# A transformer block on one core: buffer clearing moved to another engine, LayerNorm order pinned, and the feed-forward LayerNorm pulled ahead of each segment

## The chip, the cores and the metric

One core of a Trainium2 chip. TensorE (PE) multiplies matrices, with its weight loads (PEld) beside it; VectorE (DVE), ScalarE (ACT) and GpSimd (POOL) do elementwise work, and SyncE (SP) issues most of the transfers. ACT and POOL also issue transfers of their own. The metric is the device time of one execution in microseconds; lower is better. An execution takes 657.92 us before the change (median of four).

## The reference

Inputs are bfloat16: x of 2048 tokens by 576, 32 heads of 18, weights wq, wk, wv, wo (576 x 576), w1 (576 x 4608), w2 (4608 x 576). The core of it:

```python
for s in range(4):                       # four segments of L = 512 tokens
    logits = einsum('bhqd,bhkd->bhqk', qs, ks) * scale + causal_mask
    a_dot = einsum('bhqk,bhkd->bhqd', softmax(logits), vs)
    pq = phi(qs)                         # phi(t) = t + 1 if t > 0 else exp(t)
    a_mem = einsum('bhld,bhde->bhle', pq, M) / (einsum('bhld,bhd->bhl', pq, z)[..., None] + 1e-06)
    o = g * a_mem + (1.0 - g) * a_dot    # g = sigmoid(beta), one value per head
    M = M + einsum('bhld,bhle->bhde', phi(ks), vs);  z = z + einsum('bhld->bhd', phi(ks))
# q, k, v = layernorm(x) @ wq, wk, wv
h = x + concat(o) @ wo
out = h + gelu(layernorm(h) @ w1 + b1) @ w2 + b2
```

## The kernel before

**Two phases, tiles of 128 tokens.** Phase A is attention, over 16 tiles T (four a segment). Phase B is the feed-forward network (FFN), over four segments b of 512 tokens. The rows of h pass between them through `h_dram` in DRAM.

**A projection tile** (`proj_tile`): DVE takes the statistics of the tile (two `bn_stats`, one `bn_aggr`, tiles `stats` and `mv`), POOL makes `ve` (variance plus epsilon) and `rstd` (its power of -0.5), DVE makes `nmr` and then `xn`, the normalised tile. PE transposes it (`pT`), DVE copies that out, and 30 matmuls into six PSUM tiles `pq` give Q, K and V. ACT casts these into `Qp`, `Kp` (a head takes 32 columns, of which 18 are filled and the rest must be zero) and `Vp`. DVE makes relu and min of K for the memory; PE transposes Q (`ptq`) and K (`ptk`), DVE copies them to `QTt` and `KT`, and four DVE copies spread QTt into a block-diagonal `QTbd` whose other blocks must be zero. From segment 1 on, Q also meets the memory `BDp`, which gives `Rsb`.

**An attention tile** (`attention_tile`): for each pair of (head group, key tile) PE makes scores into `st` (two PSUM buffers), ACT takes the exp into `E`, POOL masks the diagonal blocks (`affine_select`), and PE multiplies with V into `pv`. `normalize` divides and adds Rsb, on DVE, into `oseg`. `wo_tile` transposes oseg, copies it (`oT`), multiplies with `wo_sb` into `ph`, adds x and writes h to DRAM.

**Order.** The code emits projections of tiles 0 to 2, then for each T: attention of T, projection of T+3, `wo_tile` of T-1. A scheduler of the framework then orders the instructions of each engine by its own estimate; each engine runs its list in order. Xn, Qp, Kp, QTbd and the FFN weights w1 and w2 are cut out of one SBUF array, so all of these are called `arena` in the profile. The zero parts are cleared once at the start, before anything is projected: Qp, Kp and two of the five QTbd buffers on DVE, three QTbd buffers and `expKp` on POOL (L132 to L143); the masks, wo's padding and oseg's padding follow on POOL (L145 to L179). ACT issues the loads of wq, beta and wo, POOL that of wk, SP that of x and wv.

**FFN.** For each segment b, and for its four tiles: load `h_t`, POOL adds the bias b2 (`hb`), DVE and POOL do the LayerNorm (`statsB`, `mvB`, `veB`, `rstdB`, `nmrB`, `hn`), PE transposes five blocks (`pT3`, printed as pT), DVE copies them into `hnT`. Then 36 ft blocks of five matmuls each, two blocks to a PSUM tile `pf` and one gelu on ACT (`g2`, printed g), then four tiles of 72 matmuls into `acc`, which DVE adds to hb and SP stores.

Of the kernel before, what the change touches and what calls it, by code (L numbers as in the profile page):

```python
# [11 lines left out]
ALU = mybir.AluOpType  # L12
# [12 lines left out]
def kernel(  # L25
# [15 lines left out]
    cfg = {"mask": "pool", "bd_eng": "dve", "ahead": 3, "wo_lag": 1}  # L41
# [27 lines left out]
    MASK = cfg.get("mask", "dve")  # L69
    PJ_BUFS = cfg.get("pj_bufs", 3)  # L70
    PV_BUFS = cfg.get("pv_bufs", 1)
    HB_ENG = cfg.get("hb_eng", "pool")
    BD_ENG = cfg.get("bd_eng", "pool")
# [7 lines left out]
    PROJ_E = NCH * 3 * D + 2 * DPAD + 4 * H * 32 + 2 * TPS * H * 32 + 2 * NCH * P + 4 * NG * P + (cfg.get('ahead', 1) + 2) * NG * 4 * P  # L81
# [13 lines left out]
    nc.gpsimd.memset(negh[:], -0.5)  # L95

    with ExitStack() as phA:
# [7 lines left out]
        epool = phA.enter_context(tc.tile_pool(name="epool", bufs=cfg.get("e_bufs", 8 if cfg.get("half_su", True) else 4)))  # L105
        psS = phA.enter_context(tc.tile_pool(name="psS", bufs=cfg.get("st_bufs", 2 if cfg.get("half_su", True) else 1), space=PSUM))
# [3 lines left out]
        NB = 2  # L110
# [9 lines left out]
        AHEAD = cfg.get("ahead", 1)  # L120
        NQ = AHEAD + 2
        QTbd_t = [carve(NG * 4 * P).rearrange("p (g j n) -> p g j n", g=NG, j=4) for _ in range(NQ)]

# [3 lines left out]
        queues = [nc.scalar, nc.gpsimd, nc.sync]  # L127
        for i, w in enumerate((A_wq, A_wk, A_wv)):
            eng = queues[i]
            eng.dma_start(wqkv[:, 0:4, i * D:(i + 1) * D], w[0:512, :].rearrange("(c p) n -> p c n", p=P))  # L130
            eng.dma_start(wqkv[0:64, 4, i * D:(i + 1) * D], w[512:576, :])
        nc.gpsimd.memset(wqkv[64:128, 4, :], 0.0)  # L132
        for i in range(NB):
            nc.gpsimd.memset(xn_t[i][:, D:DPAD], 0.0)
        for i in range(NB):
            nc.vector.memset(Qp_t[i][:], 0.0)
            nc.vector.memset(Kp_t[i][:], 0.0)
        for i in range(NQ):
            (nc.gpsimd if i % 2 == 0 else nc.vector).memset(QTbd_t[i][:], 0.0)  # L139
        Vp_t = [persX.tile([P, TPS, H, 19], BF16, name=f"Vp{i}") for i in range(NB)]  # L140
        for i in range(NB):
            nc.gpsimd.memset(Vp_t[i][:, :, :, 18:19], 1.0)
        nc.gpsimd.memset(expKp[:], 0.0)  # L143
        mask01 = consts.tile([P, P], BF16, name="mask01")
        nc.gpsimd.memset(mask01[:], 1.0)  # L145
        nc.gpsimd.affine_select(out=mask01[:], in_=mask01[:], pattern=[[1, P]], compare_op=ALU.is_ge,
                                fill=0.0, base=0, channel_multiplier=-1)
        maskneg = None
        if MASK == "pe":
            maskneg = consts.tile([P, P], BF16, name="maskneg")  # L150
            nc.gpsimd.memset(maskneg[:], 0.0)
            nc.gpsimd.affine_select(out=maskneg[:], in_=maskneg[:], pattern=[[1, P]], compare_op=ALU.is_ge,
                                    fill=-1.0e9, base=0, channel_multiplier=-1)
        bdmask = consts.tile([P, 4 * 19], F32, name="bdmask")
        nc.gpsimd.memset(bdmask[:], 1.0)
        bdv = bdmask[:, :].rearrange("p (j e) -> p j e", e=19)
        nc.gpsimd.affine_select(out=bdv, in_=bdv, pattern=[[-32, 4], [0, 19]], compare_op=ALU.is_ge,
                                fill=0.0, base=0, channel_multiplier=1)
        nc.gpsimd.affine_select(out=bdv, in_=bdv, pattern=[[32, 4], [0, 19]], compare_op=ALU.is_ge,
                                fill=0.0, base=17, channel_multiplier=-1)  # L160
        wo_sb = wX.tile([P, NCH, D], BF16, name="wo_sb")
        nc.gpsimd.memset(wo_sb[64:128, 4, :], 0.0)
        beta_sb = consts.tile([P, H], BF16, name="beta_sb")
        nc.scalar.dma_start(beta_sb[:], A_beta.partition_broadcast(P))
        nc.scalar.dma_start(wo_sb[:, 0:4, :], A_wo[0:512, :].rearrange("(c p) n -> p c n", p=P))
        nc.scalar.dma_start(wo_sb[0:64, 4, :], A_wo[512:576, :])
        G = consts.tile([P, H], F32, name="G")
        OMG = consts.tile([P, H], F32, name="OMG")
        Mst = consts.tile([P, NG, 76], F32, name="Mst")
        nc.scalar.activation(G[:], beta_sb[:], ACT.Exp, scale=-1.0)  # L170
        nc.vector.tensor_scalar_add(G[:], G[:], 1.0)
        nc.vector.reciprocal(G[:], G[:])
        nc.vector.tensor_scalar(out=OMG[:], in0=G[:], scalar1=-1.0, scalar2=1.0, op0=ALU.mult, op1=ALU.add)

        state = {}
        NO = 3
        oseg_t = [persX.tile([P, DPAD], BF16, name=f"oseg{i}") for i in range(NO)]
        for i in range(NO):
            nc.gpsimd.memset(oseg_t[i][:, D:DPAD], 0.0)  # L179
        qtp = phA.enter_context(tc.tile_pool(name="qtp", bufs=AHEAD + 2))  # L180
        rpool = phA.enter_context(tc.tile_pool(name="rpool", bufs=AHEAD + 2))
# [6 lines left out]
        def proj_tile(s, t):  # L188
# [4 lines left out]
            if t == 0:  # L193
# [8 lines left out]
            tcols = slice(t * P, (t + 1) * P)  # L202
            stats = small.tile([P, 2, 6], F32, name="stats")
            nc.vector.bn_stats(out=stats[:, 0, :], in_=x_seg[:, t, 0:288])
# [10 lines left out]
            nc.vector.tensor_scalar(out=xn[:, 0:D], in0=x_seg[:, t, :], scalar1=rstd[:, 0:1],  # L215
                                    scalar2=nmr[:, 0:1], op0=ALU.mult, op1=ALU.add)
# [21 lines left out]
            if s < NSEG - 1:  # L238
                nc.vector.tensor_scalar_max(reluKp[:, t, :], Kp[:], 0.0)
# [9 lines left out]
            for j in range(4):  # L249
                eng = nc.gpsimd if BD_ENG == "pool" else nc.vector  # L250
                eng.tensor_copy(QTbd[32 * j:32 * j + 32, :, j, :], QTt[32 * j:32 * j + 32, :, :])  # L251
# [34 lines left out]
        def mupdate(s):  # L286
            Vp = Vp_t[s % NB]
# [22 lines left out]
        HALF = cfg.get("half_su", True)  # L310

        def attention_tile(s, t):
            T = s * TPS + t
            QTt = state[("QT", T)]
# [3 lines left out]
            oseg = oseg_t[T % NO]  # L318
            bcols = [(g, kt) for g in range(NG) for kt in range(t + 1)]
            SUs = [bcols[i:i + 4] for i in range(0, len(bcols), 4)]  # L320
# [20 lines left out]
            def do_pv(g):  # L341
# [4 lines left out]
                for j in range(4):  # L346
                    h = 4 * g + j
                    hl = h - 16 * hf
                    for kt in range(t + 1):
                        E, b, slot = E_of[(g, kt, j)]  # L350
# [29 lines left out]
            for L in pairs:  # L380
# [6 lines left out]
                for b, (g, kt) in enumerate(L):  # L387
# [8 lines left out]
                    for j in range(4):  # L396
                        E_of[(g, kt, j)] = (E, b, j)
                for g in pending:
                    do_pv(g)
# [175 lines left out]
```

## Time and profile before

| | us |
|---|---|
| median of 4 runs (657.4 to 659.84) | 657.92 |
| the profiled execution | 659.19 |
| its span in the trace | 657.5 |
| mean granted clock of TensorE in it | 0.955 |

A row of the profile's groups reads: line, engine, operation, output <- input (partitions x elements, type), count | busy time in us, mean ns of one | idle time of the engine just before, and what ended it. A row of the timeline reads: start, duration (both us), engine, line, operation, count, and in brackets how long the engine had been idle before and what ended that. A row of the chain reads: start, duration, engine, tile, line, count. A row of a window reads: its limits and length, then the busy us (and count) of PE, PEld, DVE, ACT and POOL, the granted clock, the busy share of the DMA engines and their GB/s.

### The profile page before, as it was taken

The page shows a single profiled execution, that of the slowest core. Times are in us where ns is not written, and L with a number is a line of the kernel's source. Part 1 is how long each engine was busy: PE and PEld are TensorE (multiplying, and loading weights), DVE is VectorE, ACT ScalarE, POOL GpSimd, SP SyncE. Part 2 cuts the span into 40 slices and gives each one's busy share as a digit, 9 for nine tenths or more (in the row PEclk, how much of TensorE's full clock was granted, in tenths as well). Part 3 has the DMA queues.
Part 4 walks back from the last instruction along what each step waited for, and adds up shares of the span by engine and source line. Part 5 has one row for each costly group of instructions (what it writes and reads, how often), then busy time and mean ns, then how long its engine had stood idle before and what let it go on. Part 6 is the DMA issues. An engine that isn't in the chain of part 4 may idle for free.

```text
span 657.5 us, 11656 instructions
## 1 busy us (share of the span) xinstructions
PE 555.5 (84%) x4935; PEld 354.4 (54%) x4992; DVE 244.0 (37%) x630; ACT 285.4 (43%) x355; POOL 161.7 (25%) x249
## 2 busy tenths in 40 slices
PE   0488988899988897687069999799997999989997
PEld 0356555566556555453034477345773457744576
DVE  6578674877567736642361000400103001010011
ACT  0156889768966895586024400144001440034300
POOL 9642334422442234632640001200111000000000
PEclk9979999999989998898569999899997999999999
DMA  7010010000001024950310000000000000000000
GB/s 252 0 37 2 19 37 20 19 20 20 19 19 44 19 74 133 322 189 12 99 45 1 0 10 19 28 0 1 10 19 10 0 1 10 19 10 0 1 19 19
DMA packets 19190, 25.98 MB, mean 40 GB/s; under 512 B 1665, under 2 KB 17841, under 8 KB 19137
## 3 DMA queue, kind: packets, MB, share of 16 engines
q1 hardware_dynamic: 16258, 17.93, 8.8%
q0 software_dynamic: 1520, 5.97, 2.6%
q10 hardware_dynamic: 1360, 1.34, 0.6%
q8 instruction: 39, 0.64, 0.4%
q14 instruction: 13, 0.11, 0.1%
HBM read 20.51 MB, written 4.72 MB: 38 GB/s over the span
## 4 chain that ended last, share of the span: by engine, by line
PE 69%; DVE 16%; POOL 6%; ACT 6%; issue 2%; DMA 1%; SPq 0%; DVEq 0%; ACTq 0%; POOLq 0%
PE pf L527 24%; PE acc L537 22%; PE pq L226 8%; ACT E L386 5%; DVE arena L251 5%; PE st L383 5%; PE ph L417 4%; PE pv L351 3%; POOL arena L139 2%; DVE QTt L59 2%; DVE KT L59 1%; POOL hb L498 1%; DVE arena L262 1%; DVE hnT L59 1%; PE ptq L245 1%
## 5 line engine op out<-in xcount | busy, mean ns | idle before, releaser
L386 ACT ACTIVATE E<-st 128x1024 bf16<-128x1024 f32 x160 | 155.5, 1023 | 41.8 <-PE st L383 19.1
L527 PE MATMUL pf<-hnT,arena 128*128 128x512 bf16 x704 | 160.4, 387 | 4.0 <-DVE hnT L59 2.8
L530 ACT ACTIVATE g<-pf 128x1024 bf16<-128x1024 f32 x72 | 73.6, 1024 | 205.1 <-PE pf L527 205.0
L537 PE MATMUL acc<-arena,g 128*128 128x288 bf16 x1152 | 142.9, 286 | 0.0
L537 PEld LDWEIGHTS <-g 128*128 128x128 bf16 x1152 | 112.6, 98 | 30.4
L394 POOL TENSOR_SCALAR_AFFINE_SELECT E<-E 128x512 bf16<-128x512 bf16 x128 | 85.5, 679 | 150.6 <-ACT E L386 150.2
L527 PEld LDWEIGHTS <-arena 128*128 128x128 bf16 x720 | 71.8, 100 | 91.4 <-issue 10.7
L542 DVE TENSOR_TENSOR o_t<-acc,hb 128x288 bf16<-128x288 f32 x32 | 13.2, 453 | 279.2 <-PE acc L537 279.2
L383 PE MATMUL st<-arena,KT 128*128 128x512 bf16 x279 | 88.6, 384 | 13.0 <-ACT E L386 9.7
L351 PEld LDWEIGHTS <-E 128*128 128x128 bf16 x1280 | 49.9, 96 | 48.2 <-POOL E L394 16.8
L226 PE MATMUL pq<-arena 128*128 128x288 bf16 x480 | 72.9, 297 | 1.3 <-DVE arena L59 1.0
L351 PE MATMUL pv<-Vp,E 128*128 128x19 bf16 x1280 | 59.8, 173 | 10.8 <-ACT E L386 6.4
L226 PEld LDWEIGHTS <-arena 128*128 128x128 bf16 x480 | 46.4, 101 | 17.6 <-DVE arena L59 3.1
L498 POOL TENSOR_TENSOR hb<-h_t,b2bc 128x576 f32<-128x576 bf16 x16 | 20.4, 1281 | 137.0 <-DVE o_t L542 131.5
L57 ACT CAST arena<-pq 128x288 bf16<-128x288 f32 x64 | 24.5, 408 | 27.0 <-PE pq L226 27.0
L251 DVE COPY arena<-QTt 32x1024 bf16<-32x1024 bf16 x64 | 35.3, 551 | 0.6
L383 PEld LDWEIGHTS <-KT 128*128 128x128 bf16 x320 | 25.4, 97 | 17.4 <-issue 8.1
L417 PE MATMUL ph<-wo_sb,oT 128*128 128x288 bf16 x160 | 30.0, 311 | 3.3 <-DVE oT L59 2.4
L519 PE MATMUL pT<-ident,hn 128*128 128x128 bf16 x80 | 8.7, 250 | 26.8 <-DVE hnT L59 13.6
L219 PE MATMUL pT<-ident,arena 128*128 128x128 bf16 x80 | 7.5, 224 | 25.2 <-POOL rstd L211 24.5
L417 PEld LDWEIGHTS <-oT 128*128 128x128 bf16 x160 | 15.3, 105 | 13.8 <-DVE oT L59 7.3
L519 PEld LDWEIGHTS <-hn 128*128 128x128 bf16 x80 | 6.6, 111 | 29.1 <-issue 23.5
(91 smaller groups left out, 427.0 us busy)
## 6 DMA issues: line engine op xcount, KB each, us to landing
arena<-in_B_w_dram POOLq DMA_DIRECT2D x3, 864.0 KB, 5.3
arena<-in_B_w_dram SPq DMA_DIRECT2D x3, 864.0 KB, 10.3
x_seg<-in_A_x_dram SPq DMA_DIRECT2D x4, 576.0 KB, 4.7
xr<-in_A_x_dram SPq DMA_DIRECT2D x16, 144.0 KB, 2.8
h_dram<-h_sb SPq DMA_DIRECT2D x16, 144.0 KB, 1.8
arena<-in_B_w_dram POOLq DMA_DIRECT2D x3, 768.0 KB, 8.4
arena<-in_B_w_dram SPq DMA_DIRECT2D x3, 768.0 KB, 8.6
h_t<-h_dram SPq DMA_DIRECT2D x16, 144.0 KB, 2.2
```

What stands on the lines that cost most here:

```text
L59: nc.vector.tensor_copy(out_ap, in_ap)
L226: nc.tensor.matmul(pq[:], lhsT=xnT[:, c, :], rhs=wqkv[:, c, c0:c0 + 288], start=(c == 0), stop=(c == NCH - 1))
L251: eng.tensor_copy(QTbd[32 * j:32 * j + 32, :, j, :], QTt[32 * j:32 * j + 32, :, :])
L351: nc.tensor.matmul(pv[:, hl, 0:19], lhsT=E[:, b, slot * P:(slot + 1) * P], rhs=Vp[:, kt, h, :], start=(kt == 0), stop=(kt == t))
L383: nc.tensor.matmul(st[:, b, :], lhsT=KT[:, g, kt * P:(kt + 1) * P], rhs=QTbd[:, g, :, :], start=True, stop=True)
L386: nc.scalar.activation(E[:], st[:], ACT.Exp, scale=SCALE)
L394: nc.gpsimd.affine_select(out=v, in_=v, pattern=[[0, 4], [1, P]], compare_op=ALU.is_ge, fill=0.0, base=0, channel_multiplier=-1)
L417: nc.tensor.matmul(ph[:], lhsT=oT[:, c, :], rhs=wo_sb[:, c, hf * 288:(hf + 1) * 288], start=(c == 0), stop=(c == NCH - 1))
L498: nc.gpsimd.tensor_tensor(out=hb[:], in0=h_t[:], in1=b2bc[:], op=ALU.add)
L527: nc.tensor.matmul(pf[:, k, :], lhsT=w1_sb[:, c, ft * P:(ft + 1) * P], rhs=hnT[:, c, :], start=(c == 0), stop=(c == NCH - 1))
L530: nc.scalar.activation(g2[:], pf[:], ACT.Gelu_apprx_tanh)
L537: nc.tensor.matmul(acc[hf][:], lhsT=gT[ft // 2][:, ft % 2, t * P:(t + 1) * P], rhs=w2_sb[:, ft, hf * 288:(hf + 1) * 288], start=(ft == 0), ...
```

## The change

Four things move; what is computed stays.

1. **Start.** The zero fills of Qp, Kp, expKp, four and a half QTbd buffers go to ACT, as `memzero` (an activation on the buffer taken as 32-bit words); POOL keeps half of the first QTbd. wq and wv are loaded by SP, wk by POOL. Masks, the sigmoid of beta, wo's load and the pads are emitted where they are first used. A first power on POOL (`warm`) is done right at the start.
2. **LayerNorm order in attention.** The first statistics instruction of a tile and its xn get an issue-order token: the statistics of tile T+1 stand behind the xn of tile T on DVE.
3. **FFN LayerNorm ahead.** `ffn_prep(b)` does what phase B's LayerNorm did, from its own load `h_ln` of h. For b = 0 it is called inside phase A, from T = 13 on in the code's order; for b + 1 between the two matrix products of segment b. `load_hb(b)` loads h a second time for the residual and bias.
4. **Pools.** hn and hnT get pools outside of phase A; the pool of g2 gets `reuse_waits="tile"`.

```diff
-    cfg = {"mask": "pool", "bd_eng": "dve", "ahead": 3, "wo_lag": 1}
+    cfg = {"wqueues": "sgs", "prologue": 3, "prep_in_a": 1}
...
+    hnTp = ctx.enter_context(tc.tile_pool(name="hnTp", bufs=2))
...
+    warm = consts.tile([P, 2], F32, name="warm")
+    nc.gpsimd.memset(warm[:], 1.0)
+    nc.gpsimd.tensor_tensor(out=warm[:, 1:2], in0=warm[:, 0:1], in1=negh[:], op=ALU.pow)
+    hn_t = [consts.tile([P, DPAD], BF16, name=f"hn{i}") for i in range(2)]
+    hnT_of = {}
+    def ffn_prep(b, spool, wpool, pspool, pstag, first_use):
+        hnT = hnTp.tile([P, NCH, LSEG], BF16, name="hnT")
+        hnT_of[b] = hnT
+        for t in range(TPS):
+            T = b * TPS + t
+            h_t = wpool.tile([P, D], BF16, name="h_ln")
+            nc.sync.dma_start(h_t[:], h_dram[T])
...
-        queues = [nc.scalar, nc.gpsimd, nc.sync]
+        qmap = {"s": nc.sync, "a": nc.scalar, "g": nc.gpsimd}
...
-        for i in range(NB):
-            nc.vector.memset(Qp_t[i][:], 0.0)
-            nc.vector.memset(Kp_t[i][:], 0.0)
-        for i in range(NQ):
-            (nc.gpsimd if i % 2 == 0 else nc.vector).memset(QTbd_t[i][:], 0.0)
...
-        nc.gpsimd.memset(expKp[:], 0.0)
...
+            if T < NB:
+                nc.gpsimd.memset(xn[:, D:DPAD], 0.0)
+                nc.scalar.memzero(Qp[:])
+                nc.scalar.memzero(Kp[:])
+            if T == 0 and ST_MODE == "bd":
+                nc.scalar.memzero(QTbd_t[0][:, 0:4, :, :])
+                nc.gpsimd.memset(QTbd_t[0][:, 4:8, :, :], 0.0)
+                for k in range(1, NQ):
+                    nc.scalar.memzero(QTbd_t[k][:])
+                if NSEG > 1:
+                    done.add("expKp")
+                    nc.scalar.memzero(expKp[:])
...
+            if LN_TOK:
+                tc.stamp_issue_order_token(bn0.ins, "ln")
...
+            if LN_TOK:
+                tc.stamp_issue_order_token(xn_ins.ins, "ln")
...
         def attention_tile(s, t):
+            if once("attn_setup"):
...
+                nc.scalar.dma_start(beta_sb[:], A_beta.partition_broadcast(P))
+                nc.scalar.activation(G[:], beta_sb[:], ACT.Exp, scale=-1.0)
...
+        emit_proj_upto(cfg.get("prologue", 1))
         for T in range(NT):
             s, t = divmod(T, TPS)
             attention_tile(s, t)
-            if T + AHEAD < NT:
-                emit_proj(T + AHEAD)
+            emit_proj_upto(T + AHEAD + 1)
             if T - WO_LAG >= 0:
-                wo_tile(T - WO_LAG)
+                emit_wo(T - WO_LAG)
+            if T >= PREP_FROM:
+                maybe_prep()
...
+        prep_b(0)
+        for b in range(NSEG):
+            hnT = hnT_of[b]
+            hb_tiles = load_hb(b)
...
                 nc.scalar.activation(g2[:], pf[:], ACT.Gelu_apprx_tanh)
                 gT.append(g2)
+            prep_b(b + 1)
             for t in range(TPS):
```

The order that the scheduler makes, at the places where it counts. First ACT at the start of the program. Before:

```order
L130 DMA arena<-in_A_wq_dram 128x4x576
L131 DMA arena<-in_A_wq_dram 64x576
L164 DMA beta_sb<-in_A_beta_dram 128x32
L165 DMA wo_sb<-in_A_wo_dram 128x4x576
L166 DMA wo_sb<-in_A_wo_dram 64x576
L170 ACT_TABLE_LOAD
L170 ACTIVATE G<-beta_sb 128x32
L57 CAST arena<-pq 128x16x18 x4
```

and after, from the table load to the first casts:

```order
L228 ACTIVATE arena<-arena 128x2048 x4
L231 ACTIVATE arena<-arena 128x2048
L222 ACTIVATE arena<-arena 128x512
L223 ACTIVATE arena<-arena 128x512
L361 DMA beta_sb<-in_A_beta_dram 128x32
L468 DMA wo_sb<-in_A_wo_dram 128x4x576
L362 ACTIVATE G<-beta_sb 128x32
L469 DMA wo_sb<-in_A_wo_dram 64x576
L57 CAST arena<-pq 128x16x18 x4
```

The fills (L222 to L231; two of 512 words and one of 1024 stand ahead of the rows shown) now come before the load of beta, the sigmoid's exp (G) and the first casts of Q and K.

Second, DVE in the middle of attention, behind an xn (the row `arena<-x_seg,rstd,nmr`; rden, c and oseg belong to `normalize`). Before:

```order
L59 COPY arena<-pT 128x640
L215 TENSOR_SCALAR arena<-x_seg,rstd,nmr 128x576
L327 RECIPROCAL rden<-pv 128x16
L213 TENSOR_SCALAR nmr<-mv,rstd 128x1
L329 TENSOR_TENSOR c_1023<-rden,OMG 128x16
L332 TENSOR_TENSOR oseg_149<-pv,c_1023 128x288
```

and after:

```order
L59 COPY arena<-pT 128x640
L249 TENSOR_SCALAR arena<-x_seg,rstd,nmr 128x576
L235 BN_STATS stats<-x_seg 128x6
L382 RECIPROCAL rden<-pv 128x16
L241 BN_AGGR mv<-stats 128x2
L239 BN_STATS stats<-x_seg 128x6
L384 TENSOR_TENSOR c_1032<-rden,OMG 128x16
L247 TENSOR_SCALAR nmr<-mv,rstd 128x1
L387 TENSOR_TENSOR oseg_120<-pv,c_1032 128x288
L124 BN_STATS statsB<-h_ln 128x6
L125 BN_STATS statsB<-h_ln 128x6
L127 BN_AGGR mvB<-statsB 128x2
```

Each tile's statistics now stand directly behind the xn of the tile before, where they used to be taken for several tiles at once and earlier; the FFN's statistics (statsB) have come into attention.

Third, PE where attention passes into the FFN. Before, the last of the 20 transposes of segment 0 stand directly ahead of the first pf, behind the last output projection:

```order
L519 LDWEIGHTS hn_5083
L519 MATMUL pT_5174<-ident,hn_5083 128x128
L519 LDWEIGHTS hn_5083
L519 MATMUL pT_5174<-ident,hn_5083 128x128
L527 LDWEIGHTS arena
L527 MATMUL pf<-hnT,arena 128x512
```

and after, the first pf stand among the last pv:

```order
L406 LDWEIGHTS E
L406 MATMUL pv<-Vp_117,E 128x19
L596 LDWEIGHTS arena
L596 MATMUL pf<-hnT,arena 128x512
L596 LDWEIGHTS arena
L596 MATMUL pf<-hnT,arena 128x512
L596 LDWEIGHTS arena
L596 MATMUL pf<-hnT,arena 128x512
L406 LDWEIGHTS E
L406 MATMUL pv<-Vp_117,E 128x19
```

Behind these come 13 pv, 8 pf, the three last transposes of oseg, 3 pf, the ten ph of the last tile, and 166 pf to the first acc. The transposes of segment 0 now lie inside attention, and those of the next segments stand in fives between the first acc of the segment before, with five acc in between.

More of the change, by code (lines that the diff above doesn't have):

```diff
@@ L143 @@
-        nc.gpsimd.memset(expKp[:], 0.0)
[L144 to L173, printed above, removed]
-        state = {}
[L176 to L179, printed above, removed]
@@ L481, with prep_b, load_hb @@
         nc.vector.tensor_copy(b2bc[:], b2tmp[:])
-        NBh = 2
-        hn_t = [persB.tile([P, DPAD], BF16, name=f"hn{i}") for i in range(NBh)]
-        for i in range(NBh):
-            nc.gpsimd.memset(hn_t[i][:, D:DPAD], 0.0)
-            nc.gpsimd.memset(hn_t[i][:, D:D + 1], 1.0)
-        for b in range(NSEG):
-            hnT = workB.tile([P, NCH, LSEG], BF16, name="hnT")
-            hb_tiles = []
+        def prep_b(b):
+            if b < NSEG and b not in hnT_of:
+                ffn_prep(b, smallB, lnB, psT, None, first_use=(len(hnT_of) == 0))
+        def load_hb(b):
+            tiles = []
             for t in range(TPS):
```

260 lines of the change are left out of this document (164 added, 96 removed).

## The prediction

> **What bounds the kernel now.** I read the page's busy shares and slices first, then the chain of waits, then three stretches of the timeline.
>
> ```profile
> PE 555.5 (84%) x4935; PEld 354.4 (54%) x4992; DVE 244.0 (37%) x630; ACT 285.4 (43%) x355; POOL 161.7 (25%) x249
> PE   0488988899988897687069999799997999989997
> PEclk9979999999989998898569999899997999999999
> PE 69%; DVE 16%; POOL 6%; ACT 6%; issue 2%; DMA 1%; SPq 0%; DVEq 0%; ACTq 0%; POOLq 0%
> ```
>
> PE is busy 84% of the span and carries 69% of the chain. Its slices are low in three kinds of places: at the very start, at slices 18 to 20 (296 to 345 us), and in single slices later. The change works on exactly these, so I price each from its own rows.
>
> **The start.** Timeline rows (start, duration, engine):
>
> ```profile
> 0.97 0.48 DVE L136 MEMSET arena<- 128x512 uint32 x1 [0.97 <-PEq L559]
> 3.32 1.53 POOL L132 MEMSET arena<- 64x1728 bf16 x1
> 5.08 10.45 POOL L139 MEMSET arena<- 128x4096 bf16 x3
> 22.08 0.74 POOL L209 TENSOR_SCALAR ve<-mv 128x1 f32<-128x1 f32 x4
> 22.79 2.13 POOL L211 TENSOR_TENSOR rstd<-ve,negh 128x1 f32<-128x1 f32 x4
> 24.52 0.71 PE L219 MATMUL pT<-ident,arena 128*128 128x128 bf16 x5 [24.52 <-POOL rstd L211]
> 25.90 4.97 PE L226 MATMUL pq<-arena 128*128 128x288 bf16 x30 [0.67 <-DVE arena L59]
> 27.32 0.40 ACT L57 CAST arena<-pq 128x288 bf16<-128x288 f32 x1 [16.05 <-PE pq L226]
> 34.32 0.82 PE L383 MATMUL st<-arena,KT 128*128 128x512 bf16 x2 [1.89 <-DVE arena L251]
> ```
>
> PE first works at 24.52, because the LayerNorm of tile 0 waits for POOL, and POOL clears buffers until 22 us. The first Q/K/V eviction (the cast) stands at 27.32, the first score matmul at 34.32, 7.0 us later. The change clears the same buffers on ACT instead: four of 512 four-byte words, one of 1024, five of 2048 in each partition. No row shows such a fill; the nearest give a straight line:
>
> ```profile
> L386 ACT ACTIVATE E<-st 128x1024 bf16<-128x1024 f32 x160 | 155.5, 1023 | 41.8 <-PE st L383 19.1
> L57 ACT CAST arena<-pq 128x288 bf16<-128x288 f32 x64 | 24.5, 408 | 27.0 <-PE pq L226 27.0
> 8.31 1.28 ACT L170 ACT_TABLE_LOAD   x1 [8.31 <-DMA arena<-in_A_wq_dram]
> xr<-in_A_x_dram SPq DMA_DIRECT2D x16, 144.0 KB, 2.8
> ```
>
> From 288 to 1024 elements is 0.615 us, so 0.836 ns an element and 0.17 us fixed: 0.60, 1.02 and 1.88 us for the three sizes, 4 x 0.60 + 1.02 + 5 x 1.88 = 12.8 us. DVE begins its first fill at 0.97, with nothing of the program ahead of it; if ACT does the same and loads its table in 1.28 us, it has cleared at 15.0. Behind that stands the load of beta (the order puts it there), and the sigmoid's exp waits for it: 2.8 us as for a quiet transfer, then 0.2 for the exp and 0.5 to issue the last wo load, so the first cast comes at 18.5 instead of 27.32, **a gain of 8.8 us**. PE is not later than that: POOL keeps the weights' pad (to 4.9), half of one buffer (10.45 / 3 / 2 = 1.7) and small things of about 0.8 ahead of the variance and the power (0.2 and 0.5 by the x4 rows), so rstd is there at 8.1 instead of 23.3, and pq, which now stands 2.6 behind it, can start near 11, three PSUM buffers ahead of the casts. From cast to first score I keep the 7.0 us. The moves of wq and wv onto SP, and of wo behind the fills, cost nothing: the casts come later than a 2.8 us transfer needs, and wo is needed only by the first output projection, behind a whole attention tile. Bounds: if a four-byte word costs ACT twice as much, the cast comes at 31.3 and the start loses 4.0 us; if something hides the fills entirely, pq at 11 instead of 25.9 is worth 14.9 us. I take the line between the two ACT rows, the nearest; DVE's 0.48 for 512 words says that such a fill needn't be slower.
>
> [...]
>
> **The handover to the FFN.** Timeline rows, and from the chain in order of time those with matmul counts and no bracket:
>
> ```profile
> 306.67 0.49 PE L351 MATMUL pv<-Vp,E 128*128 128x19 bf16 x13 [0.52 <-POOL E L394]
> 308.19 0.46 DVE L338 TENSOR_TENSOR oseg<-a,Rsb 128x288 bf16<-128x288 f32 x1
> 318.25 3.76 POOL L498 TENSOR_TENSOR hb<-h_t,b2bc 128x576 f32<-128x576 bf16 x3 [5.41 <-DMA h_t<-h_dram]
> 309.24 0.49 DVE L59 COPY oT<-pT 128x640 bf16<-128x640 bf16 x1 [0.60 <-PE pT L410]
> 309.79 2.58 PE L417 MATMUL ph<-wo_sb,oT 128*128 128x288 bf16 x10 [0.58 <-DVE oT L59]
> 335.48 0.58 PE L527 MATMUL pf<-hnT,arena 128*128 128x512 bf16 x1 [1.03 <-DVE hnT L59]
> 135.88 1.31 PE ph L417 x10
> 429.81 10.74 PE pf L527 x49
> 376.57 35.46 PE acc L537 x287
> ```
>
> Attention ends at 307.2, yet the first FFN matmul (pf) starts at 335.5: h goes to DRAM and back, POOL adds the bias ahead of the LayerNorm of four tiles, and PE is idle for most of 28 us. Then 180 pf run until the second FFN product (acc) starts at 376.57. In the change, segment 0's LayerNorm, transposes and hnT are done inside attention, so pf needs only a PSUM pair that the exp releases, and weights that landed earlier: DMA is down to 59 GB/s at 290 to 295 us (below). Working forward on the order's rows, at 10.74 / 49 = 0.219 us for each pf: pv ends at 307.2; 8 pf to 308.9; 3 transposes of oseg (it is ready at 308.65) to 309.4; 3 pf while DVE copies oT, to 310.1; ph x10 at 1.31 to 311.4; 166 pf at 36.4 to 347.8. I add 1.0 for the gelu table load and a slow clock, 348.8. **376.6 - 348.8 = 27.8 us gained.** Bounds: ph at its 2.58 us of the slow clock and 14 pf at double time leave 23; no addition at all leaves 29.
>
> **The three segment boundaries.** Four chain rows, of which the first stands above:
>
> ```profile
> 457.60 35.46 PE acc L537 x287
> 539.52 35.46 PE acc L537 x287
> 618.35 35.46 PE acc L537 x287
> 413.33 0.44 PE L519 MATMUL pT<-ident,hn 128*128 128x128 bf16 x5 [1.13 <-DVE hnT L59]
> 576.28 0.44 PE L519 MATMUL pT<-ident,hn 128*128 128x128 bf16 x5 [0.91 <-DVE hnT L59]
> ```
>
> From the end of one acc run to the start of the next is 45.6, 46.5 and 43.4 us; 180 pf take 39.5 of each, which leaves 6.1 + 7.0 + 3.9 = 17.0 us. There PE does 20 transposes and waits in between for DVE's copy and the next hn. The change puts the same transposes, in fives, between the first acc matmuls of the segment before, and DVE has its first two hn ready long since. Each five cost 0.44 us; five acc take 0.62 us (35.46 / 287 each), against DVE's copy and hn, so about 2.0 us a boundary. **17.0 - 6.0 = 11.0 us gained.** Bounds: no cover at all, 3 x 3.9, leaves 5.3; free transposes give 17.0.
>
> ```profile
> 416.90:421.00 4.10, 4.04 (x11) 1.54 (x12) 2.46 (x9) 0.06 (x1) 0.98 (x3) 0.58 0.04 13
> 498.40:502.40 4.00, 3.75 (x9) 1.43 (x10) 0.31 (x1) 0.00 (x0) 0.00 (x0) 0.50 0.02 4
> 579.30:583.00 3.70, 3.60 (x16) 1.66 (x17) 0.00 (x0) 1.02 (x1) 0.00 (x0) 1.00 0.00 0
> 290.00:295.00 5.00, 4.32 (x53) 2.28 (x51) 1.88 (x6) 4.46 (x5) 1.85 (x3) 1.00 0.20 59
> ```
>
> In these stretches (busy time by engine, then granted clock, DMA share, GB/s) the clock after the first two boundaries was 0.58 and 0.50, after the third 1.00; that is why the third costs 3.9 and not 6 or 7. [...]
>
> **Inside attention** the change costs something. LayerNorm of each tile now comes right behind that of the tile before, instead of up to eight ahead, and segment 0's FFN LayerNorm comes on top.
>
> ```profile
> 194.78 0.43 DVE L239 TENSOR_SCALAR arena<-arena 128x1024 bf16<-128x1024 bf16 x1 [3.31 <-ACT arena L57]
> 23.39 0.21 DVE L213 TENSOR_SCALAR nmr<-mv,rstd 128x1 f32<-128x1 f32 x1 [3.46 <-POOL rstd L211]
> 24.05 0.76 DVE L215 TENSOR_SCALAR arena<-x_seg,rstd,nmr 128x576 bf16<-128x576 bf16 x2
> L505 DVE BATCH_NORM_STATS2 statsB<-h_t 128x6 f32<-128x288 bf16 x16 | 6.8, 427 | 0.0
> L511 POOL TENSOR_TENSOR rstdB<-veB,negh 128x1 f32<-128x1 f32 x16 | 9.3, 582 | 2.4 <-DVE hn L515 1.1 <-DVE nmrB L513 0.5
> ```
>
> Behind the normalised tile DVE is idle 3.3 us while PE makes Q, K and V. A LayerNorm there is two stats of 0.43, two small DVE steps of 0.2 (nmr's row), and about 1.0 waiting on POOL (0.58 and the variance's 0.2, with signals): 2.3 us, covered. The FFN's adds as much DVE work (1.26), its hn (0.38 as for xn), its copy (0.49 as for oT) and some 0.8 of waiting: 2.9. Where both fall in one slot (two tiles), 1.9 us stick out: 3.8. Behind DVE then wait the relu of K, QTt, and PE's scores. The other two are split up, and 20 more transposes lie where ACT sets the pace. The normalisation that sometimes stands behind the POOL wait holds up pv by under 1 us. Together **4.0 us lost**; bounds -3 (shorter bursts of stats help) and +15 (12 tiles at about 1.2 us).
>
> **The sum** against the profiled execution of 659.19 us: 659.2 - 8.8 - 27.8 - 11.0 + 4.0 = 615.6. The profiled execution lies 1.3 above the median of 657.92; so 614.3, and I say 615.
>
> **The rivals.** (a) Attention pays: DVE in order behind POOL, which is in order behind masks that wait for ACT, holds each of 12 tiles, +11 us over mine: 626. Against it: the 3.3 us of idle. 15%. (b) The ACT fills are slow and the start is lost: 615 + 8.8 + 3, up to 627; for it, no row shows a fill. 10%. (c) The boundaries keep a slow clock or uncovered transposes: 621, by the range 5.3 above; 8%. (d) The start is better (pq hides the fills) and the interior free: 615 - 5.5 - 5 = 605; 10%. (e) The change does not do what it says at the handover: the first pf is held behind something that ends with attention (weights, a buffer), and half of 27.8 stays: 629; 3%. (f) Slower than before: the same wait as in (a), at all 16 tiles, outlasting cover; it decides from 43 / 16 = 2.7 us a tile beyond the idle slot, which a mask row of 0.65 us and 2.3 us of LayerNorm can't reach unless each also waits a whole exp behind ACT; 662, 2%. My forecast has 52%, its own range 609 to 621.
>
> **The numbers.** 603 to 629 takes in (a) to (d) and leaves about 1 in 8 outside. About 0.3%, 2 us, is what a measurement of this kernel can tell from no change; faster 0.97, same 0.01, slower 0.02.
>
> **What would show it.** First cast near 18 and first score near 25 us; pf before the last pv and acc starting some 37 us earlier in the span; less than 42 us from acc to acc; DVE's idle behind xn nearly gone. I am wrong if ACT's fills run past 20 us, or if attention from first score to last pv takes over 280 us (now 273).

## The result and the profile after

The changed kernel takes 603.25 us (median of 11 runs, 600.06 to 606.49) against 658.49 us before (15 runs): a ratio of 0.9167, 95% interval 0.9144 to 0.9189, so 55 us faster. I had said 615 (603 to 629): the direction and the places were right, the gain was a fifth too small, and the time lies at the very edge of the range. The profiled execution took 604.32 us, its span 602.6. From its page the busy shares, the slices and the chain by engine:

```profile
PE 545.8 (91%) x4935; PEld 350.7 (58%) x4992; DVE 236.4 (39%) x624; ACT 297.0 (49%) x365; POOL 150.0 (25%) x248
PE   2788988899978987689899999999999999999997
PEclk9899999999998999889999999999999999999999
PE 70%; DVE 17%; ACT 7%; issue 3%; POOL 3%; DVEq 0%; ACTq 0%; POOLq 0%
```

PE does the same matmuls and is busy 91% of the span instead of 84%. From slice 19 on its clock stays at 9 tenths or more, and its busy share too, apart from slice 20 and the last one. The timeline of the start:

```profile
0.79 1.28 ACT L222 ACT_TABLE_LOAD   x1 [0.79 <-PEq L629]
2.08 0.63 ACT L222 ACTIVATE arena<-arena 128x512 uint32<-128x512 uint32 x1
4.08 1.89 ACT L228 ACTIVATE arena<-arena 128x2048 uint32<-128x2048 uint32 x1
4.94 0.42 ACTq L361 DMA_DIRECT2D beta_sb<-in_A_beta_dram  x1
8.13 0.59 POOL L245 TENSOR_TENSOR rstd<-ve,negh 128x1 f32<-128x1 f32 x1
11.62 5.05 PE L262 MATMUL pq<-arena 128*128 128x288 bf16 x30 [0.58 <-DVE arena L59]
13.60 0.61 ACT L223 ACTIVATE arena<-arena 128x512 uint32<-128x512 uint32 x1
14.24 0.98 ACT L57 CAST arena<-pq 128x288 bf16<-128x288 f32 x3
21.22 0.59 PE L423 MATMUL st<-arena,KT 128*128 128x512 bf16 x1 [1.31 <-DVE arena L289]
```

The first score stands at 21.22 instead of 34.32. Beta's load goes out at 4.94, in the middle of the fills, and the first casts follow the last fill at once. The handover, five transposes between the first acc at the first boundary, and the first acc behind the two others:

```profile
293.56 0.81 PE L596 MATMUL pf<-hnT,arena 128*128 128x512 bf16 x2
294.23 0.49 PE L406 MATMUL pv<-Vp,E 128*128 128x19 bf16 x13
296.31 1.28 ACT L599 ACT_TABLE_LOAD   x1 [2.84 <-PE pf L596]
334.55 0.78 PE L607 MATMUL acc<-arena,g 128*128 128x288 bf16 x5
411.25 0.44 PE L142 MATMUL pT<-ident,hn 128*128 128x128 bf16 x5
411.53 0.78 PE L607 MATMUL acc<-arena,g 128*128 128x288 bf16 x5
412.27 0.44 PE L142 MATMUL pT<-ident,hn 128*128 128x128 bf16 x5
487.45 0.78 PE L607 MATMUL acc<-arena,g 128*128 128x288 bf16 x5
563.09 1.63 PE L607 MATMUL acc<-arena,g 128*128 128x288 bf16 x12
```

The first pf stand ahead of the last pv, and the transposes stand among the acc without a gap. Between the marks that the prediction used, in us:

| stretch | before | after | gain | forecast |
|---|---|---|---|---|
| to the first score | 34.32 | 21.22 | 13.1 | 8.8 |
| first score to the last pv's end | 272.8 | 273.5 | -0.7 | -4.0 |
| last pv to the first acc | 69.4 | 39.8 | 29.6 | 27.8 |
| first to fourth acc run | 241.8 | 228.5 | 13.2 | 11.0 |
| from there to the end | 39.2 | 39.5 | -0.4 | 0 |

The gains sum to 54.9, the difference of the spans (657.5 - 602.6).

### The profile page after: what moved, and what is told of

It is laid out like the page before. It is cut to its first block, busy times and chain, and to the rows that moved or that the text cites. A ratio compares the mean times of both kernels' runs of the same rounds, so it can differ in the third digit from the quotient of the medians.

```text
span 602.6 us, 11691 instructions
## 1 busy us (share of the span) xinstructions
PE 545.8 (91%) x4935; PEld 350.7 (58%) x4992; DVE 236.4 (39%) x624; ACT 297.0 (49%) x365; POOL 150.0 (25%) x248
## 4 chain that ended last, share of the span: by engine, by line
PE 70%; DVE 17%; ACT 7%; issue 3%; POOL 3%; DVEq 0%; ACTq 0%; POOLq 0%
PE pf L596 26%; PE acc L607 21%; PE pq L262 7%; ACT E L425 7%; DVE arena L289 6%; PE st L423 4%; PE pv L406 4%; PE ph L482 4%; DVE QTt L59 2%; DVE KT L59 2%; DVE arena L300 1%; PE pT L142 1%; PE ptq L283 1%; PE R L307 1%; PE R L309 1%
## 5 line engine op out<-in xcount | busy, mean ns | idle before, releaser
L425 ACT ACTIVATE E<-st 128x1024 bf16<-128x1024 f32 x160 | 155.5, 1023 | 42.2 <-PE pv L406 17.6
L599 ACT ACTIVATE g<-pf 128x1024 bf16<-128x1024 f32 x72 | 73.7, 1024 | 193.0 <-PE pf L596 193.0
L596 PE MATMUL pf<-hnT,arena 128*128 128x512 bf16 x703 | 155.2, 379 | 0.9
L607 PE MATMUL acc<-arena,g 128*128 128x288 bf16 x1152 | 144.6, 286 | 0.9 <-DVE o_t L612 0.9
L596 PEld LDWEIGHTS <-arena 128*128 128x128 bf16 x720 | 70.2, 98 | 83.5
L423 PE MATMUL st<-arena,KT 128*128 128x512 bf16 x280 | 89.7, 387 | 11.9 <-ACT E L425 8.8
L406 PEld LDWEIGHTS <-E 128*128 128x128 bf16 x1280 | 49.9, 96 | 45.3 <-POOL E L433 16.4
L612 DVE TENSOR_TENSOR o_t<-acc,hb 128x288 bf16<-128x288 f32 x32 | 13.1, 452 | 152.9 <-PE acc L607 81.5
L262 PE MATMUL pq<-arena 128*128 128x288 bf16 x480 | 70.7, 291 | 0.9 <-DVE arena L59 0.6
L262 PEld LDWEIGHTS <-arena 128*128 128x128 bf16 x480 | 45.5, 99 | 16.7 <-DVE arena L59 2.7
L59 DVE COPY hnT<-pT 128x640 bf16<-128x640 bf16 x16 | 7.7, 490 | 90.6 <-PE pT L142 90.6
L482 PE MATMUL ph<-wo_sb,oT 128*128 128x288 bf16 x160 | 28.4, 298 | 2.5 <-DVE oT L59 1.8
L307 PE MATMUL R<-BDp,arena 128*128 128x76 bf16 x96 | 10.8, 210 | 12.0 <-DVE arena L300 11.9
L129 POOL TENSOR_SCALAR veB<-mvB 128x1 f32<-128x1 f32 x16 | 3.6, 223 | 67.7 <-DVE mvB L127 67.6
```

Of the source, the lines that this page charges most:

```text
L59: nc.vector.tensor_copy(out_ap, in_ap)
L262: nc.tensor.matmul(pq[:], lhsT=xnT[:, c, :], rhs=wqkv[:, c, c0:c0 + 288], start=(c == 0), stop=(c == NCH - 1))
L406: nc.tensor.matmul(pv[:, hl, 0:19], lhsT=E[:, b, sl * P:(sl + 1) * P], rhs=Vp[:, kt, h, :], start=(kt == 0), stop=(kt == t))
L423: nc.tensor.matmul(st[:, b, :], lhsT=KT[:, g, kt * P:(kt + 1) * P], rhs=QTbd[:, g, :, :], start=True, stop=True)
L425: nc.scalar.activation(E[:], st[:], ACT.Exp, scale=SCALE)
L482: nc.tensor.matmul(ph[:], lhsT=oT[:, c, :], rhs=wo_sb[:, c, hf * 288:(hf + 1) * 288], start=(c == 0), stop=(c == NCH - 1))
```

## The experiments

All times below stand beside runs of the kernel before on the same chip; a difference to the changed kernel is that of the ratios, times 658 us. Ratios are given with their intervals.

**Beta's load behind the fills.**

```diff
+                nc.scalar.memzero(beta_sb[:])
                 nc.scalar.dma_start(beta_sb[:], A_beta.partition_broadcast(P))
```

> The changed kernel, but the load of beta is made to wait for the last fill on ACT (a small fill of beta's own tile stands ahead of it). My forecast counted 3.5 us for this wait; in the changed kernel's trace the load goes out at 4.94 us, while ACT still fills until 14.1. Theory 1 (the first casts set the first score, and the beta wait was the term that was too large): fills end at 14.2, issue 0.4, transfer 2.8, exp 0.2, so the casts behind the exp stand near 17.7 instead of 14.9 and the first score near 24 instead of 21.2: 2.5 to 3.5 us slower, about 606. Rival (the normalised tile on DVE and POOL sets the first score, the casts have slack): less than 0.7 us.

Measured 603.41 us, ratio 0.9175 (0.9141 to 0.9209): 0.5 us, no difference. The first cast came at 15.31, the first score at 22.28, 1.1 us later, and the last pv at the same time as in the changed kernel. The scheduler put the sigmoid's exp behind two casts here, so the wait that I had counted, ahead of all casts, wasn't reproduced in full; first cast and first score came later by the same 1.1 us, so the casts do set the first score, against the rival's reason, but 1 us there is taken up in attention.

**The fills back on DVE and POOL.**

```diff
-                nc.scalar.memzero(Qp[:])
+                nc.vector.memset(Qp[:], 0.0)
...
```

Kp goes to DVE as well, the five QTbd in turn to POOL and DVE, expKp to POOL.

> The changed kernel with the fills of Qp, Kp, QTbd and expKp back on DVE and POOL, all else (late masks, LayerNorm token, queues) kept. Theory 1 (the gain at the start is POOL's fills ahead of the first power): POOL fills 3 x 3.48 + 3.81 us ahead of rstd instead of 1.8, rstd at 21 instead of 8.7, first score 12 to 13 us later, 615 to 617. Rival (late setups and the LayerNorm order made most of the 13 us): 4 us or less, at most 608.

Measured 616.69 us, ratio 0.9369 (0.9346 to 0.9393): 13.3 us slower. The first pq stood at 23.67 and the first score at 33.26, 12.0 later. This is theory 1: POOL's fills ahead of the first power made the late start.

**No LayerNorm order.** One setting: `"ln_tok": False`.

> The changed kernel without the LayerNorm order (statistics again taken up to eight tiles ahead). Theory 1 (the order matters little; the casts wait for ACT's fills): DVE does 16 statistics of 0.37 us ahead of the first xn, so pq starts near 14 to 16 instead of 11.6, the casts near 15.5 to 17 instead of 14.2, and the first score 1 to 3 us later; inside attention no change beyond 1 us: 604 to 607. Rival A (the order costs inside attention, as forecast): attention gets some 2 us or more shorter and makes this up, 602 or less. Rival B (the order is what keeps attention short): 608 or more.

Measured 612.0 us, ratio 0.9306 (0.9279 to 0.9333): 9.1 us slower, which neither of my lines for the start had. Its timeline:

```profile
14.43 0.46 DVE L235 BATCH_NORM_STATS2 stats<-x_seg 128x6 f32<-128x288 bf16 x1 [6.17 <-DMA x_seg<-in_A_x_dram]
17.32 0.32 DVE L247 TENSOR_SCALAR nmr<-mv,rstd 128x1 f32<-128x1 f32 x2
18.04 0.71 PE L255 MATMUL pT<-ident,arena 128*128 128x128 bf16 x5 [18.04 <-DVE arena L249]
```

The scheduler puts the statistics of the second segment ahead of tile 0's nmr. DVE, in order, sits 6.17 us on the load of that segment, and PE starts at 18.04 instead of 10.32. Attention itself took 272.9 us (first score 28.31, last pv to 301.22) against 273.5. So rival B's size came about, at another place: the order is worth 7 us at the start and nothing that shows inside (the two profiled executions lie 6.8 us apart, the medians 9.1; the other 2 lie within what executions of one kernel differ by).

**Both back.** Both edits together.

> The changed kernel with both parts of the start undone: fills back on DVE and POOL, and no LayerNorm order. One undone alone costs 13 (fills) and 9 us (order). Theory 1 (two blocks beside each other ahead of the first xn, POOL's fills and DVE's statistics that wait for the second segment's load; the later one decides): as with the fills alone, 615 to 618. Rival (the two add up): 624 to 627.

Measured 617.3 us, ratio 0.9385 (0.9354 to 0.9416): 14.3 us slower than the changed kernel, not 22. The two blocks, POOL's fills and DVE's statistics, lie beside each other; either one alone gives back most of the start. The first score stood at 35.73 here and at 34.32 before the change, so what else the change does at the start (queues, late masks, the early power) brings nothing by itself.

**The next segment's LayerNorm at its own start.**

```diff
-            prep_b(b + 1)
+            prep_b(b)          # ahead of the first product of segment b
```

> The changed kernel with the FFN LayerNorm and transposes of segments 1 to 3 emitted at the start of their own segment instead of between the two products of the one before. Theory 1 (all of the 13.2 us at the boundaries comes from the transposes being fed into the acc matmuls, without which PE waits and its clock falls): 11 to 14 us slower, 614 to 617, and the granted clock behind at least two boundaries is 0.5 to 0.6 again. Rival (the separate load and the order on POOL, free of the bias add, made half of it): boundaries of 3.9 us at full clock, 6 to 8 us slower, 609 to 611.

Measured 615.39 us, ratio 0.9356 (0.9333 to 0.9379): 12.4 us slower. The timeline at its first boundary, and, apart, a window behind the second, in which the clock fell (busy PE, PEld, DVE, ACT, POOL, then clock, DMA share, GB/s):

```profile
371.68 0.44 PE L142 MATMUL pT<-ident,hn 128*128 128x128 bf16 x5 [0.91 <-DVE hnT L59]
373.21 0.44 PE L142 MATMUL pT<-ident,hn 128*128 128x128 bf16 x5 [1.09 <-DVE hnT L59]
375.25 2.10 PE L597 MATMUL pf<-hnT,arena 128*128 128x512 bf16 x8 [0.58 <-DVE hnT L59]
```

```profile
453.00:457.00 4.00, 2.64 (x11) 1.24 (x12) 3.18 (x9) 0.00 (x0) 0.76 (x2) 0.73 0.29 78
```

This is theory 1 in size: from the first to the fourth acc run it takes 239.3 us, of the 13.2 us gained 10.7 are lost again. But the clock fell at one boundary only (0.73; 1.00 in the windows at the other two), against theory 1. At the first boundary, at full clock, the four waits for DVE are 3.2 us; from the end of an acc run to the next, 180 pf included, it takes 43.6, 45.3 and 43.1 us. So the waits between the transposes are the main price, and the fallen clock some 2 us at one boundary.

**Segment 0's LayerNorm behind attention.** One setting: `"prep_in_a": 0`.

> The changed kernel with the FFN LayerNorm of segment 0 behind attention again (that of segments 1 to 3 stays between the products). Theory 1 (segment 0's LayerNorm costs attention next to nothing, since DVE and POOL have room for it): from the first score to the last pv 273 us as in the changed kernel (273.5), while the first pf comes some 20 to 26 us behind the last pv (28.3 before the change, less POOL's bias adds ahead of it): 621 to 629. Rival (it costs attention the 4 us that I forecast): attention 269 to 270.5, and 617 to 624.

Measured 632.23 us, ratio 0.9608 (0.9592 to 0.9624): 29.0 us slower, above both lines. Attention took 271.8 us, 1.7 less than in the changed kernel; the first pf stood 28.7 us behind the last pv. Its timeline shows two causes: h_ln is loaded only when attention has ended (the next run shows that it waits for memory there), and POOL's bias adds stand between the powers:

```profile
301.31 0.46 DVE L566 CAST b2bc<-b2tmp 128x576 f32<-128x576 bf16 x1 [2.56 <-DMA b2tmp<-in_B_b_dram]
304.16 0.46 DVE L124 BATCH_NORM_STATS2 statsB<-h_ln 128x6 f32<-128x288 bf16 x1 [2.39 <-DMA h_ln<-h_dram]
307.83 3.81 POOL L580 TENSOR_TENSOR hb<-h_t,b2bc 128x576 f32<-128x576 bf16 x3
313.03 0.56 POOL L131 TENSOR_TENSOR rstdB<-veB,negh 128x1 f32<-128x1 f32 x1
321.75 0.59 PE L596 MATMUL pf<-hnT,arena 128*128 128x512 bf16 x1 [1.35 <-DVE hnT L59]
```

**The same, with its pools opened ahead of attention.**

```diff
+    lnB = ctx.enter_context(tc.tile_pool(name="lnB", bufs=4))        # and smallB
     hnTp = ctx.enter_context(tc.tile_pool(name="hnTp", bufs=2))
```

> As the run without the FFN LayerNorm in attention's code (632.2 us), but the pools of its loads and small tiles are opened ahead of attention, so that they need not wait for memory that attention gives back; the order then has the loads of h and the statistics of segment 0 inside attention, and only the 20 transposes and four copies, which need PSUM of phase B, behind it. Theory 1 (most of the handover's loss was the wait for memory, then the load, the statistics and POOL's bias adds among them; transposes and copies are 1.0 to 1.5 us a tile): first pf 8 to 10 us behind the last pv instead of 28.7, 610 to 615. Rival (the place in the code decides, whatever the pools): 628 or more.

Measured 613.88 us, ratio 0.9340 (0.9309 to 0.9372): 17.6 us of the 29 come back from the pools alone. The first pf stood 10.9 us behind the last pv, a little over the 8 to 10 that I had expected. The 20 transposes and their copies, now at 294.38 to 299.54, remain behind attention; the first of them waits for h_sb of the last tile, whose data it doesn't read; I take this for the wait for PSUM that attention gives back:

```profile
294.38 0.69 PE L144 MATMUL pT<-ident,hn 128*128 128x128 bf16 x5 [0.55 <-DVE h_sb L486]
299.54 1.87 PE L596 MATMUL pf<-hnT,arena 128*128 128x512 bf16 x4 [0.58 <-DVE hnT L59]
```

**The pool of g2 without reuse by tile.** `reuse_waits="tile"` removed; the order on every engine stays.

> The changed kernel without reuse_waits="tile" on the pool of g2: the order on each engine is the same, but the first gelus wait for more of attention's instructions on POOL and DVE. Theory 1 (what they wait for has ended by then): within 0.5 us, 602.5 to 604.5. Rival (the first gelu waits for the last output projection's additions, which end near 299.1, 1.5 us behind the gelu's start, and PE for the gelu): 604.5 to 606.

Measured 610.44 us, ratio 0.9274 (0.9255 to 0.9293): 7.0 us slower, where I had expected nothing, or by the rival 1.3 to 2.8 us. The table load and the gelu wait for DVE's conversion of b2, whose load is issued only when attention ends, and PE idles 4.80 us with both pf buffers full:

```profile
302.09 1.28 ACT L599 ACT_TABLE_LOAD   x1 [8.87 <-DVE b2bc L566]
304.46 2.29 PE L596 MATMUL pf<-hnT,arena 128*128 128x512 bf16 x5 [4.80 <-ACT g L599]
```

**An own start, first try.** Fills moved further (to DVE while it waits for x), fewer of them, 64 contraction rows in the last block of Q/K/V and 65 in that of w1, so that their pads need no fill.

> A version of the changed kernel: the last contraction block of Q/K/V takes 64 rows and that of w1 65, so that the fills of wqkv's and w1's unused rows fall away on POOL (1.53 us ahead of the first power, 4 us beside the spreading of Q late in attention, where that took DVE 3.3 instead of 0.8 us); expKp isn't cleared, since the min of all of Kp writes every column; DVE clears Qp, Kp and the first QTbd while it waits for x, ACT only four QTbd; beta is loaded first. Theory 1 (what stands ahead of the first power on POOL and of the first cast on ACT is the start): POOL's power near 6.9 instead of 8.1, first pq near 9.5 to 10, first cast near 11, first score near 18; 2 to 3 us there and 2 us late in attention: 598 to 600. Rival (the start's gain is swallowed by attention, as in the run with beta behind the fills, where a first score 1.1 us later cost nothing): only the 2 us late in attention, 601 to 602.

Measured 622.41 us, ratio 0.9448 (0.9420 to 0.9476): 18.5 us slower than the changed kernel. x landed at 7.44 instead of 4.94, with beta's load issued beside it (whether that delayed x wasn't isolated); the first score stood at 25.37, and attention took 287.4 us. The next run isolates the second loss.

**64 rows alone.**

```diff
+                        kr = D - 512 if c == NCH - 1 else P
-                        nc.tensor.matmul(pq[:], lhsT=xnT[:, c, :], rhs=wqkv[:, c, c0:c0 + 288],
+                        nc.tensor.matmul(pq[:], lhsT=xnT[0:kr, c, :], rhs=wqkv[0:kr, c, c0:c0 + 288],
```

> The changed kernel in which the last contraction block of Q/K/V takes 64 rows instead of 128 (the fill of the unused rows stays; nothing else differs). The version with an own start had attention 13.8 us longer and its first 30 pq at 8.62 us instead of 5.05. Theory 1 (the 64-row block is why: behind it the next weight load no longer lies under the matmul, 0.81 instead of 0.62 us for five at full clock): attention 10 to 16 us longer, 614 to 621. Rival (that version lost its time at the start alone, by the late x and the early sigmoid, and attention by the order that followed): within 3 us of the changed kernel, 602 to 606.

Measured 620.42 us, ratio 0.9426 (0.9400 to 0.9452): 17.0 us slower, attention 287.8 us. This is theory 1, and the groups by shape show where. First come two rows of this run (weight loads of Q/K/V), then one of the changed kernel, then w1's loads, of 65 rows in the next version and of 128 in the changed kernel, and last the timeline of this run's weight loads around its chains:

```profile
L263 PEld LDWEIGHTS <-arena 64*128 64x128 bf16 x96 | 8.9, 93 | 23.2 <-issue 22.9
L263 PEld LDWEIGHTS <-arena 128*128 128x128 bf16 x384 | 31.0, 100 | 20.2 <-DVE arena L59 3.4 <-issue 1.2
```

```profile
L262 PEld LDWEIGHTS <-arena 128*128 128x128 bf16 x480 | 45.5, 99 | 16.7 <-DVE arena L59 2.7 <-issue 0.5
```

```profile
L598 PEld LDWEIGHTS <-arena 65*128 65x128 bf16 x144 | 14.0, 97 | 16.9
L596 PEld LDWEIGHTS <-arena 128*128 128x128 bf16 x720 | 70.2, 98 | 83.5
```

```profile
188.63 0.58 PEld L263 LDWEIGHTS <-arena 64*128 64x128 bf16 x5 [0.24 <-issue]
189.45 0.58 PEld L263 LDWEIGHTS <-arena 64*128 64x128 bf16 x5 [0.24 <-issue]
191.92 0.09 PEld L263 LDWEIGHTS <-arena 64*128 64x128 bf16 x1 [0.24 <-issue]
192.15 0.23 PEld L284 LDWEIGHTS <-arena 128*128 128x128 bf16 x4
```

Ahead of the 96 loads of 64 rows the weight path sat idle 22.9 us with nothing to wait for that the profile shows, 0.24 us each; ahead of the changed kernel's 480 loads it was 16.7 us, 0.03 each. I read this as a load that doesn't go under the matmul of 128 rows ahead of it; the trace shows the idle time, not its reason. A load of 128 rows behind one of 64 starts 0.23 us after it, too (191.92 and 192.15), where loads of 128 rows in the changed kernel start 0.12 apart (30 in 3.55 us). So both changes of size cost time, not only the one behind that theory 1 names: a chain of five takes 0.82 us (188.63 to 189.45) instead of 0.61 (30 matmuls in 3.85 us). The 144 loads of 65 rows show no more idle time than w1's loads of 128 rows, 0.12 us each. But w1's matmuls have 512 columns and those of Q/K/V 288; 65 rows in Q/K/V, or 64 in w1 alone, weren't run.

**An own start, second try.** Q/K/V with 128 rows, w1 with 65; DVE fills wqkv's pad, the first Qp, Kp and QTbd while x is under way; expKp isn't filled, since the min of all of Kp writes every column of it; beta on SP behind the weights; DVE's part of the sigmoid behind the third xn.

> A second version of the changed kernel: w1's last block takes 65 rows (no fill of unused rows late in attention), Q/K/V keeps 128 rows. DVE clears wqkv's unused rows, Qp and Kp of tile 0 and the first QTbd before x lands; ACT clears four QTbd and the second Qp and Kp; expKp isn't cleared (the min of K writes all of it); beta is loaded by SP behind the weights, and DVE's part of the sigmoid stands behind the third xn. Theory 1 (POOL's list ahead of the first power and ACT's fills ahead of the first cast are the start): x at 5 us as in the changed kernel, power at 7.1, first pq near 10, first cast near 11.3, first score 19.5 to 20; QTbd's spreading late in attention 1.7 instead of 4.7 us: 597 to 600. Rival (attention takes up the start's gain, and PE has other work in that late place): 601 to 604.

Measured 597.28 us, ratio 0.9092 (0.9067 to 0.9118): 4.9 us faster than the changed kernel, the intervals apart, and the best here. The first pq stood at 10.19, the first score at 20.00. So only 1.2 us of the gain lie at the start; attention took 266.7 us instead of 273.5. Part of that is w1's 65 rows, as the next run shows, and part the clock (0.98 on the mean over attention, 0.96 in the changed kernel).

**Only w1's 65 rows.**

> The changed kernel with only one of the two parts of the version with an own start: w1's last contraction block takes 65 rows, so that POOL's fill of the unused rows (3.93 us at 248.6) falls away; the start is the changed kernel's. The four copies that spread Q there took DVE 5.38 us beside the fill and 1.80 us without it. Theory 1 (PE waits for these copies): 2 to 3.5 us faster than the changed kernel, 600 to 601.5, the start of the other version being worth 3 to 4. Rival (PE has other work there): within 1 us of the changed kernel, 602.5 to 604.

Measured 600.65 us, ratio 0.9117 (0.9083 to 0.9151): 3.3 us by the ratios, theory 1's size, though the intervals touch. DVE's spreading of Q late in attention: in the changed kernel all four copies, the first of them, and the POOL fill beside them, then the four in this run:

```profile
249.37 5.38 DVE L289 COPY arena<-QTt 32x1024 bf16<-32x1024 bf16 x4
249.37 3.42 DVE L289 COPY arena<-QTt 32x1024 bf16<-32x1024 bf16 x1
248.58 3.93 POOL L492 MEMSET arena<- 64x4608 bf16 x1
```

```profile
249.05 1.95 DVE L289 COPY arena<-QTt 32x1024 bf16<-32x1024 bf16 x4
```

5.38 us became 1.95. The first copy took 3.42 us beside the fill, from 249.37 to 252.79, where the fill ends at 252.51; the median of that trace's 64 copies is 0.42 us. So the first copy lasts until just behind the fill's end; why it does, no run here shows.

## Why the prediction was right, and where it was off

The places and their mechanisms were right, but all four terms erred the same way: 4.3 us at the start, 3.3 in attention, 1.8 at the handover, 2.2 at the boundaries. Nothing cancelled, and the time fell out of my own 609 to 621, close to rival (d) with its 605, to which I had given 10%. Of (d)'s reasons the nearly free attention came about; that pq hides the fills came about only in part, since the first casts still stood right behind the last fill.

**The start (8.8 forecast, 13.1 measured).** The fills were priced right: 0.63 and 0.61 us for 512 words and 1.89 for 2048, forecast 0.60 and 1.88. The last ended at 14.2 instead of 15.0, since each began some 0.1 us before the one ahead of it had ended (the second at 2.62, the first done at 2.71). The step that failed is "the sigmoid's exp waits for" beta's load behind the fills: 3.5 us that didn't exist, since that load was issued with six fills ahead of it not yet begun, and landed 6.7 us later, still under the fills. It went out when x had landed (4.94, as DVE's first statistics), whose semaphore it waits for, and not behind the fills. How many instructions a load may pass, no run here tests. The first cast was 4.3 us earlier than forecast (0.8 by the fills, 3.5 by this wait), and that is the whole difference. The step had a second gap: I credited the fills alone. The runs show two conditions, fills off POOL (13.3 us if undone) and the LayerNorm order (9.1 if undone, 14.3 for both), and I had priced the order only as a loss inside attention. In the trace of before, DVE's statistics up to 19.9 us stood under POOL's fills; what stands under a wait that is removed was the question I didn't ask there.

**The handover (27.8, 29.6).** Right in mechanism: 29.0 us when undone. The term that was too large is the 1.0 added for the table load and a slow clock, which is over half of the 1.8 us; the window from the last pv to the first acc has a clock of 1.00, and the table load (296.31 to 297.59) lay beside PE's pf and ph. What I passed over is the condition in part 4 of the change: without reuse by tile 7.0 us of this gain go.

```profile
294.72:334.43 39.71, 39.50 (x189) 18.36 (x192) 10.90 (x34) 18.69 (x18) 14.81 (x20) 1.00 0.31 90
```

**The boundaries (11.0, 13.2).** Right in mechanism, 12.4 us when undone. The mis-sized term is the 2.0 us left a boundary, of which 1.3 remained ((17.0 - 13.2) / 3): five transposes and five acc take 1.02 us together (411.25 to 412.27), 0.61 of it acc, so 0.4 for the transposes, and the waits for DVE that I allowed for weren't there. Rival (c) asked for a slow clock or uncovered transposes; neither came.

**Attention (4.0 lost, 0.7 measured).** The cover that I forecast is there: ahead of the 12 relus of K, DVE idled 14.5 us for ACT's casts before the change, 3.3 in the changed kernel and 11.9 without the LayerNorm order, so each tile's statistics fill that time. How much sticks out isn't settled. Undoing the order left 272.9 us, undoing segment 0's LayerNorm 271.8, both in place 273.5: 0.6 and 1.7 us by single profiles. But in the run with early pools, whose profiled execution was its fastest (610.11), attention took 267.4 us though the order and the statistics were in it; only the 20 transposes stood outside. One difference lies in the clock: its mean over attention is 0.96 in the changed kernel and 0.99 in that run. One place, first the changed kernel, then that run (columns as above):

```profile
22.00:27.00 5.00, 4.97 (x32) 3.47 (x32) 1.83 (x7) 3.03 (x6) 2.00 (x4) 0.79 0.47 121
```

```profile
22.00:27.00 5.00, 4.61 (x48) 3.77 (x46) 2.68 (x9) 3.71 (x8) 1.99 (x4) 1.00 0.46 121
```

PE was busy for most of both windows and did 32 matmuls in the one and 48 in the other. Early in attention (the ninth of the 160 exps) that run is 1.5 us ahead, at the end 6.1. Executions of one kernel differ as much: the 11 of the changed kernel spread over 6.4 us, the fastest with a mean clock of 0.994, the two slowest with 0.980. That moves this stretch by more than the terms I summed. So the cost is small, rivals (a) and (f) fell, and how much of the 0.7 is which term stays open.

## What to carry to other kernels

An engine that works its list in order can hide a second block behind the first: before crediting a removed wait, read what stands next on every engine that feeds the same instruction, and take the later of the two, not the sum (here 13.3 and 9.1 us for one undone, 14.3 for both). At the border of two phases, look for what waits on memory given back rather than on data; here pools opened earlier were worth 17.6 us and one reuse rule 7.0. Before counting a transfer as waiting for the long instructions ahead of it in a compute engine's list, see whether it depends on them: here one went out at 4.94 us with six fills still to begin, and at 14.35 once it had to wait for a fill of its own tile (14.12 to 14.32).

## What the runs showed of the hardware

In Q/K/V's chains of five matmuls, 64 instead of 128 contraction rows in the last one made a chain take 0.82 us instead of 0.61, so some 0.1 us lost at each of the two changes of size; 96 such chains made the kernel 17.0 us slower. With 65 rows in w1's chains, whose matmuls have 512 instead of 288 columns, no such loss shows: 0.12 us idle ahead of a load, as with 128 rows.

A DVE copy of 32 partitions by 1024 took 3.42 us beside a POOL fill, where the median of the 64 in that run is 0.42; four took 5.38 beside the fill and 1.95 in the run without it.

In the changed kernel the granted clock was 0.79 over 22 to 27 us, after PE had been busy 2.6 of the 6 us from 16 to 22, its longest gap there 1.91 us. In the run with early pools, with PE busy 3.7 of the same 6 us, it was 1.00 in both stretches. What sets it, no run here isolates.
